# A single-core transformer block in split fp32: sums of W4's fourth pair of chunks made during the projections, those of the fifth one step sooner, with a new table of order

## The chip, the cores and the metric

One core of one Trainium2 chip runs the whole program. The metric is the device time of one execution in microseconds (us). The core has five engines that run side by side, each through its own queue in order: TensorE (PE in the profile; PEld is its loading of weights), VectorE (DVE), ScalarE (ACT), GpSimd (POOL) and SyncE (SP), which here only issues transfers. Matmuls write into PSUM banks; VectorE and ScalarE read them from there.

## The reference

The input has S = 2048 rows of D = 512, all in fp32. With `xn = layernorm(x)`:

```
q, k, v = split(xn @ wqkv)                      # 32 heads of 16
phi(t)  = where(t > 0, t + 1, exp(t)) + 1e-6
s = (phi(q) @ (phi(k)^T v)) / (phi(q) . sum(phi(k)) + 1e-6) @ wo
# B(x), on xn:
h  = gelu(layernorm(x) @ w1)                    # 4 groups of columns, moved by +1, -1, +2, -2 rows
x1 = x + shifted(h) @ w2
B  = x1 + gelu(layernorm(x1) @ w3) @ w4         # w3: 512 x 1376, w4: 1376 x 512
out = x + s * silu(B(xn))
```

## The kernel before, in words

**Arithmetic.** Each fp32 operand is split into a high part `h` (rounded on ScalarE) and a low part `l` (the difference, on VectorE). A product is three matmuls, high·high, low·high, high·low. Nearly all matmuls stand on one line, L146; activations are L168, two-tensor operations L191 and L201, operations with one tensor L196, loads L207, stores L212 and L214, fetches from the kernel's own DRAM buffers L219, gathers L225. Large products go by a scheme of seven products instead of eight (`seven`, L929): the quarters of one operand and sums of them (`a11`, `s1`, ...) are multiplied by quarters and sums of the other (`b11`, `t1`, ... `t4`). It uses three PSUM banks: `pa` once; `pe` for the product with `t1` and then, on top of it, with `b22`; and `pb` four times on top of each other, for `b11`, `t2`, `t3`, `t4`. Between two products in one bank another engine reads the partial sum: ScalarE copies `p1` and `u2` from `pb` and `p5` from `pe`, VectorE forms the third result from `pb + p5`. The next product into the bank must wait for that read, since it adds to what was read.

**Stages** (us of the profiled execution). Tiles are 128 rows, 16 of them; four make a block, four blocks. 0–54: layernorm sums, key, query and the Gram matrix of the first block (the column sums `ksum` and `qsum` of the weights, multiplied by ones, serve the layernorm). 54–129: keys and queries of blocks 1 to 3 (`pair_kq`, two tiles at a time), from sums of the transposed input's chunks. 129–230: first and second mixing product (`w1`, `w2`) and the shift. 230–291: block 0 through `w3` (`up_pair`, five pairs of chunks, s = 0 to 4, of 128 columns each) and, in plain matmuls into four accumulating banks `acc`, through `w4` (`down`). 291–405: blocks 1 to 3 through `w3` (`up_late`), with the attention products between (their banks end in `s`: `pbs`, `pes`). 405–492: blocks 2, 3 and 1 through `w4` by the scheme of seven (`down_late`), banks `pbd`, `ped`. Then the last output rows leave.

**The sums in question.** `down_late` needs the sums `t1` to `t4` of W4's pairs of chunks (s and s + 5). `sums_w4(s)` (L1190) makes them for one pair: two loads `wr` of 256 KB, four VectorE operations over 256 columns (`wt`), two high parts on ScalarE, two low parts on VectorE, and four stores of 256 KB to DRAM (`wtd`), from where `fetch_w4` brings them back later. Pair 0's are made in block 2's projections, those of 1 and 2 in block 3's. The dictionary `SUMS` names the (block, pair) of the `w3` stage after which those of pairs 3 and 4 are made.

**What sets the order.** The code above doesn't issue instructions: it records operations in a `Plan` (L79 on). `emit` (L285) then goes through them as a list scheduler with durations of its own: on each engine it takes, of the operations that could start soonest there, the one with the earliest due time. Due times follow from TensorE's recorded order; the table `SOONER` at the program's end shifts the due time of single operations, given as pairs (number of the operation in order of recording, shift in units of 0.25 us). What comes out is a fixed queue for each engine, and where each tile lies. A tile's number in a name counts tiles and differs between two programs for the same thing.

Of the kernel before, what the change touches and what calls it, by code (L numbers as in the profile page):

```python
# [411 lines left out]
def linear_attn_gated_by_mixer(  # L412
# [33 lines left out]
    SUMS = {(3, 1): (3,), (3, 3): (4,)}  # L446
# [1200 lines left out]
    for b in range(1, NQ):  # L1647
# [17 lines left out]
        if b == 3:  # L1665
            sums_w4(1)
# [47 lines left out]
    b = 2  # L1714
# [24 lines left out]
    b = 3  # L1739
# [29 lines left out]
    for b in range(NQ):  # L1769
        if b in LATE:  # L1770
            up_last(b)
            for s in range(NS):
# [3 lines left out]
                attends((b, s))  # L1776
                for k in SUMS.get((b, s), ()):
                    sums_w4(k)
# [3 lines left out]
        for n, fs in enumerate(groups):  # L1782
# [15 lines left out]
            attends((b, n))  # L1798
            for s in SUMS.get((b, n), ()):
                sums_w4(s)  # L1800
# [13 lines left out]
    for b in LINE:  # L1814
# [121 lines left out]
```

## Time and profile before

| what | us |
|---|---|
| runs | 498.06, 498.6, 498.03 |
| median | 498.06 |
| profiled execution | 498.08 |
| its span in the profile | 496.4 |
| TensorE busy | 490.6 |
| VectorE busy | 438.4 |
| ScalarE busy | 373.4 |

The span runs from the first to the last recorded instruction; the rest of an execution lies around it. Busy time is the sum of an engine's instructions. For matmuls the start is recorded and the end is modelled, so that two of them overlap in the rows; the time from one start to the next tells what TensorE got through. In a row of the timeline stand the start, the duration, engine, line, operation, output and inputs, and in brackets the idle time ahead of it with what ended it.

### The profile page before, as it was taken

Reading aid. Unit: us, or ns where it says so; the run is one execution under the profiler, and the core shown is the slowest. Engines: PE = TensorE matmul, PEld = TensorE weight load, DVE = VectorE, ACT = ScalarE, POOL = GpSimd, SP = SyncE. Lnnn points to the kernel's source line nnn. Section 1 sums busy time; section 2 is a strip of 40 time slices with the busy share of each in tenths; the row PEclk is TensorE's granted clock in tenths of the full one; section 3 lists DMA queues with packets and bytes.
Section 4 is the critical chain, followed back from the end, with each engine's and each line's share of the span. In section 5 each row is a group of like instructions: output and inputs, shape, how many; then the busy total and the mean of one; then the engine's idle time right before and its main releaser. Section 6 shows DMA issues by size and latency. Waiting matters only on the chain.

```text
span 496.4 us, 9885 instructions
## 1 busy us (share of the span) xinstructions
PE 490.6 (99%) x3244; PEld 447.0 (90%) x3244; DVE 438.4 (88%) x874; ACT 373.4 (75%) x845; POOL 123.6 (25%) x214
## 2 busy tenths in 40 slices
PE   8999999999999999999999999999999999999996
PEld 6778888888888999899889999999999999999996
DVE  5998997889989669999999999999999899796864
ACT  5999999677887599999988567765686877565531
POOL 1384404276930232133200021100000000143420
PEclk9999999999999999999999999999999999999999
DMA  7869696999974999999988499984634699599996
GB/s 229 303 187 297 133 296 183 237 287 269 329 220 100 236 310 248 273 252 290 337 268 247 158 194 298 247 262 138 183 114 147 215 336 332 114 226 283 278 224 182
DMA packets 87082, 117.44 MB, mean 237 GB/s; under 512 B 10328, under 2 KB 39160, under 8 KB 87032
## 3 DMA queue, kind: packets, MB, share of 16 engines
q1 hardware_dynamic: 75512, 96.11, 59.6%
q0 software_dynamic: 11520, 20.71, 24.9%
q8 instruction: 25, 0.41, 0.4%
q14 instruction: 25, 0.20, 0.1%
HBM read 72.66 MB, written 39.93 MB: 227 GB/s over the span
## 4 chain that ended last, share of the span: by engine, by line
PE 97%; DMA 1%; SPq 1%; ACT 0%; DVE 0%; issue 0%; ACTq 0%
PE pb L146 12%; PE pbd L146 9%; PE h L146 9%; PE g L146 9%; PE acc L146 6%; PE pe L146 6%; PE pbx L146 6%; PE ped L146 5%; PE pbm L146 5%; PE pbs L146 5%; PE q L146 3%; PE pa L146 3%; PE pex L146 3%; PE k L146 3%; PE pad L146 3%; PE pes L146 2%
## 5 line engine op out<-in xcount | busy, mean ns | idle before, releaser
L225 POOL DMA_DIRECT2D xo<-x1d x12 | 10.9, 950 | 166.2 <-DVE xo L191 118.5
L225 POOL DMA_DIRECT2D th<-in_x x14 | 12.2, 895 | 45.0 <-DVE th L201 23.1
L225 POOL DMA_DIRECT2D o<-xnd x16 | 14.0, 887 | 37.5 <-DVE o L191 13.5
L168 ACT ACTIVATE th<-xo 128x512 f32<-128x512 f32 (+1 forms) x16 | 9.7, 614 | 15.9 <-DVE xo L201 10.1
L225 POOL DMA_DIRECT2D zacc<-ke x12 | 12.9, 1073 | 31.4 <-DMA zacc<-ke 10.4
L191 DVE TENSOR_TENSOR ht<-h,abc 128x512 f32<-128x512 f32 x16 | 11.0, 690 | 7.5 <-PE h L146 7.4
L225 POOL DMA_DIRECT2D xt<-nrow x16 | 14.6, 1288 | 8.4 <-ACT k12h L168 4.1
L196 POOL TENSOR_SCALAR w<-mv 128x4 f32<-128x4 f32 (+2 forms) x10 | 2.5, 254 | 40.7 <-ACT sq L168 40.4
L168 ACT ACTIVATE y<-o,nm,rs 128x512 f32<-128x512 f32 x16 | 12.4, 814 | 0.2 <-POOL nm L196 0.2
L168 ACT ACTIVATE p<-pb 128x256 f32<-128x256 f32 x20 | 7.6, 381 | 5.8 <-PE pb L146 5.4
L168 ACT ACTIVATE ht<-ht 128x512 f32<-128x512 f32 x16 | 10.0, 626 | 2.1 <-DVE ht L191 2.0
L168 ACT ACTIVATE sq<-o,mv 128x512 f32<-128x512 f32 x16 | 11.5, 722 | 0.1
L168 ACT ACTIVATE u<-pb 128x256 f32<-128x256 f32 x20 | 7.7, 383 | 5.1 <-PE pb L146 4.5
L201 DVE SCALAR_TENSOR_TENSOR pq<-pq,rd 128x512 f32<-128x512 f32 x16 | 11.0, 688 | 0.3
L168 ACT ACTIVATE p<-pe 128x256 f32<-128x256 f32 x20 | 7.7, 384 | 4.6 <-PE pe L146 4.1
L201 DVE SCALAR_TENSOR_TENSOR qz<-pq,zb 128x512 f32<-128x512 f32 x16 | 10.8, 682 | 0.0
L1471 DVE TENSOR_REDUCE den<-qz 128x32 f32<-128x512 f32 x16 | 10.8, 679 | 0.0
L168 ACT ACTIVATE sq<-o 128x512 f32<-128x512 f32 x16 | 10.0, 629 | 0.1
L613 POOL TENSOR_TENSOR rs<-w,nhalf 128x4 f32<-128x4 f32 (+2 forms) x10 | 9.7, 970 | 0.8
L168 ACT ACTIVATE x<-x,nm,rs 128x512 f32<-128x512 f32 x12 | 9.2, 805 | 0.0
L201 DVE SCALAR_TENSOR_TENSOR th<-th,so 128x512 f32<-128x512 f32 x12 | 8.2, 683 | 0.6 <-ACT th L168 0.5
L168 ACT ACTIVATE sq<-x,mv 128x512 f32<-128x512 f32 x12 | 8.6, 718 | 0.1
(2075 smaller groups left out, 2446.9 us busy)
## 6 DMA issues: line engine op xcount, KB each, us to landing
w_s<-in_w SPq DMA_DIRECT2D x28, 256.0 KB, 5.6
x<-in_x SPq DMA_DIRECT2D x16, 256.0 KB, 6.2
xt<-in_xt SPq DMA_DIRECT2D x16, 256.0 KB, 6.9
xnd<-x SPq DMA_DIRECT2D x16, 256.0 KB, 5.9
xt<-nrow POOLq DMA_DIRECT2D x16, 256.0 KB, 7.6
pqd<-qr SPq DMA_DIRECT2D x16, 256.0 KB, 6.1
o<-xnd POOLq DMA_DIRECT2D x16, 256.0 KB, 6.6
x1d<-o SPq DMA_DIRECT2D x16, 256.0 KB, 5.1
```

The lines of the kernel that those rows point to most:

```text
L146: lambda: nc.tensor.matmul(out.get(), lhs.get(), rhs.get(), start=start, stop=stop, skip_group_check=more))
L168: nc.scalar.activation(out.get(), src.get(), func, scale=get(scale), **kw)
L191: self.vec(eng, out, [a, b], lambda: self.e(eng).tensor_tensor(out.get(), a.get(), b.get(), op=op), True)
L196: lambda: self.e(eng).tensor_scalar(out.get(), a.get(), get(s1), get(s2), **kw), False,
L201: lambda: self.nc.vector.scalar_tensor_tensor(out.get(), a.get(), get(s), b.get(), op0=op0, op1=op1),
L225: lambda: self.nc.gpsimd.dma_start(out.get(), get(src), accum_op=ALU.add), mb=mb)
L613: lambda: g.tensor_tensor(out.get(), src.get(), nh.get(), op=ALU.pow))
L1471: pl.add("DVE", .6, .68, [t], [den], lambda: nc.vector.tensor_reduce(den.get(), t.get().rearrange("p (h d) -> p h d", d=DH), axis=AX.X, op ...
```

## The change

`sums_w4(3)` moves from the stage of block 3's second pair (row (3, 1) of `SUMS`) into the projections: in the loop over blocks it is recorded in block 2's turn at the place where block 3's turn records `sums_w4(1)`, ahead of the second `pair_kq`. `sums_w4(4)` moves from (3, 3) to (3, 2). The table `SOONER` is replaced as a whole (longer by seven lines, so L1931 becomes L1938). The operations and the matmuls are the same ones.

```diff
-    SUMS = {(3, 1): (3,), (3, 3): (4,)}
+    SUMS = {(3, 2): (4,)}
...
-        if b == 3:
-            sums_w4(1)
+        if b > 1:
+            sums_w4(3 if b == 2 else 1)
         pair_kq(t0 + 1)
...
     SOONER = (
-        25, 43, 34, 17, 48, 11, 52, 22, 57, 4, 63, 3, 76, 3, 88, -164, 90, 14, 91, -77, 94, 30, 95, 2, 96, 3,
...
+        5418, 25, 5444, -19, 5471, 28, 5478, -18, 5496, -37, 5531, 47,
     )
```

**The sums of pair 3 on VectorE.** VectorE's queue in block 2's projections, near 80 us, before (`ke`, `qk`, `qi`, `qr`, `zi` are key and query intermediates, `x8` a normalised tile):

```order
L201 SCALAR_TENSOR_TENSOR qr_1071<-qe_1040,qk_881 128x512
L201 SCALAR_TENSOR_TENSOR qk_1078<-pbx_943,ns_94,p5x_1068 128x512
L201 SCALAR_TENSOR_TENSOR qi_1095<-pex_979,rs_92,u2x_1021 128x512
L201 SCALAR_TENSOR_TENSOR ke_1102<-ke_1102,zi_1043 128x512
L191 TENSOR_TENSOR x8l<-x_432,x8h 128x512
L201 SCALAR_TENSOR_TENSOR k8l<-ke_1102,k8h 128x512
L201 SCALAR_TENSOR_TENSOR ke_1135<-ke_1135,zk_1117 128x512
```

and now:

```order
L191 TENSOR_TENSOR wt_1099<-wr_974 128x256
L201 SCALAR_TENSOR_TENSOR qr_1113<-qe_1103,qk_892 128x512
L201 SCALAR_TENSOR_TENSOR ke_1110<-ke_1110,zi_1071 128x512
L191 TENSOR_TENSOR x8l<-x_337,x8h 128x512
L201 SCALAR_TENSOR_TENSOR wt_1099<-wt_1099,wr_999 128x256
L191 TENSOR_TENSOR wt_1144<-wr_999,wr_974 128x256
L201 SCALAR_TENSOR_TENSOR wt_1144<-wt_1099,wr_999 128x256
L201 SCALAR_TENSOR_TENSOR k8l<-ke_1110,k8h 128x512
L191 TENSOR_TENSOR wt_31l<-wt_1144,wt_31h 128x512
L191 TENSOR_TENSOR wt_30l<-wt_1099,wt_30h 128x512
L201 SCALAR_TENSOR_TENSOR ke_1173<-ke_1173,zk_1123 128x512
```

The four sums and the two low parts stand between the key work of tiles 8 and 9.

**Block 0's third pair on TensorE.** The pair s = 2 of block 0, bank `pb0_2`, where the product with `t3` (left factor `yt30`, weights named `w3_2_s1`) is followed by that with `t4` (left factor `yt40`, weights `w3_2_b`); `acc` are the plain products with `w4`. TensorE's queue before, near 253 us:

```order
L146 MATMUL pb0_2_3539<-yt30h_3046,w3_2_s1h_3492 128x256
L146 MATMUL pb0_2_3539<-yt30l_3180,w3_2_s1h_3492 128x256
L146 MATMUL pb0_2_3539<-yt30h_3046,w3_2_s1l_3505 128x256
L146 MATMUL acc0_3_3296<-w4_0_1h_3230,f0_1l_3495 128x512
L146 MATMUL acc0_2_3277<-w4_0_6h_3311,f0_6h_3482 128x512
L146 MATMUL acc0_1_3330<-w4_0_1h_3230,f0_1h_3476 128x512
L146 MATMUL acc0_1_3330<-w4_0_1l_3306,f0_1h_3476 128x512
L146 MATMUL pb0_2_3539<-yt40h_3146,w3_2_b_3055 128x256
L146 MATMUL pb0_2_3539<-yt40l_3192,w3_2_b_3055 128x256
```

and now:

```order
L146 MATMUL pb0_2_3495<-yt30h_3152,w3_2_s1h_3571 128x256
L146 MATMUL pb0_2_3495<-yt30l_3196,w3_2_s1h_3571 128x256
L146 MATMUL pb0_2_3495<-yt30h_3152,w3_2_s1l_3583 128x256
L146 MATMUL pb0_2_3495<-yt40h_3194,w3_2_b_3594 128x256
L146 MATMUL pb0_2_3495<-yt40l_3209,w3_2_b_3594 128x256
```

The four `acc` matmuls between the two products stand elsewhere; three such matmuls now stand ahead of `t3`, between it and `t2`.

**The first Gram matmuls.** TensorE's queue near 18 us before (`k` is the last key product, `g` the Gram products of the first tile):

```order
L146 MATMUL k_151<-wk_3h,u_3h 128x512
L146 MATMUL k_151<-wk_3l,u_3h 128x512
L146 MATMUL k_151<-wk_3h,u_3l 128x512
L146 MATMUL qsum<-wqt,ones 128x512
L146 MATMUL g_304<-k0h,x0h 128x512
L146 MATMUL g_310<-k0h,x0h 128x512
```

and now:

```order
L146 MATMUL k_160<-wk_3h,u_3h 128x512
L146 MATMUL k_160<-wk_3l,u_3h 128x512
L146 MATMUL k_160<-wk_3h,u_3l 128x512
L146 MATMUL g_295<-k0h,x0h 128x512
L146 MATMUL g_297<-k0h,x0h 128x512
```

`qsum` moves behind the first nine `g` matmuls. On ScalarE, whose `k0h` the `g` matmuls need, the queue ahead of it was

```order
L168 ACTIVATE wneg<-ksum 128x512
L168 ACTIVATE wq_2h<-wq_s_165 128x512
L168 ACTIVATE wq_0h<-wq_s_169 128x512
L168 ACTIVATE kr_261<-kt_247,rs_92 128x512
L168 ACTIVATE kt_247<-kt_247,rs_92 128x512
L168 ACTIVATE wq_1h<-wq_s_181 128x512
L168 ACTIVATE sq_281,mv_90<-x_194 128x512
L168 ACTIVATE k0h<-kr_261 128x512
```

and is now

```order
L168 ACTIVATE wneg<-ksum 128x512
L168 ACTIVATE sq_248,mv_90<-x_178 128x512
L168 ACTIVATE kr_257<-kt_246,rs_92 128x512
L168 ACTIVATE kt_246<-kt_246,rs_92 128x512
L168 ACTIVATE x0h<-x_134 128x512
L168 ACTIVATE wq_1h<-wq_s_195 128x512
L168 ACTIVATE k0h<-kr_257 128x512
```

The square of the second `x` tile (`sq`) stands ahead of `kr`, and `x0h` ahead of `k0h`.

135 rows, old and new, of the table SOONER are left out of this document.

## The prediction

> **What bounds the kernel now.** I read the page first, then the waits of TensorE, the table by stage, and last the rows of single places. On the page:
>
> ```profile
> PE 490.6 (99%) x3244; PEld 447.0 (90%) x3244; DVE 438.4 (88%) x874; ACT 373.4 (75%) x845; POOL 123.6 (25%) x214
> PE 97%; DMA 1%; SPq 1%; ACT 0%; DVE 0%; issue 0%; ACTq 0%
> ```
>
> TensorE is busy for 490.6 of the span's 496.4 us, and the chain of work that ended last is 97% TensorE. The waits of TensorE (engine, line, what was waited for, us in all, times, longest):
>
> ```profile
> PE warm L146 <- POOL ones L529: 1.1, 1, 1.1
> PE k L146 <- DVE u_1l L191: 0.4, 1, 0.4
> ```
>
> So after the first microsecond one wait is listed. The same matmuls are issued before and after the change, so it can only move time between matmuls: what is to be gained is what TensorE waits now, and what is to be lost are waits that a new order makes. VectorE's cover, by stage (bounds; duration; busy us and instructions of PE, PEld, DVE, ACT, POOL; clock; DMA share; GB/s):
>
> ```profile
> 78.00:87.00 9.00, 9.00 (x41) 7.21 (x40) 5.61 (x9) 8.86 (x21) 5.52 (x11) 1.00 0.45 118
> 97.00:101.00 4.00, 4.00 (x19) 3.25 (x18) 1.25 (x4) 1.57 (x3) 1.02 (x2) 1.00 1.08 349
> 112.00:129.00 17.00, 17.00 (x75) 13.78 (x74) 16.25 (x30) 13.61 (x25) 12.11 (x28) 1.00 1.06 297
> 230.00:291.00 61.00, 61.00 (x391) 54.95 (x390) 60.17 (x119) 50.12 (x119) 6.58 (x11) 1.00 0.82 250
> 330.00:373.00 43.00, 42.93 (x361) 42.62 (x360) 42.49 (x91) 27.75 (x74) 0.00 (x0) 1.00 0.57 160
> 373.00:405.00 32.00, 32.00 (x271) 31.93 (x270) 28.61 (x62) 23.29 (x60) 0.00 (x0) 1.00 0.69 218
> ```
>
> VectorE has 3.39 of 9 us free in 78–87 and 2.75 of 4 in 97–101, but under 1 us of 61 in 230–291. The clock column says 1.00 throughout.
>
> The span's end is not touched. The last matmul starts at 491.79, one ScalarE and two VectorE operations follow, then the store; the new order ends with the same ones (start, duration, of the first two):
>
> ```profile
> 491.79 0.28 PE L146 MATMUL pbd<-w_l1h,dl1l 96*128 96x256 f32 x1
> 492.10 0.38 ACT L168 ACTIVATE th<-pbd 128x256 f32<-128x256 f32 x1 [1.16 <-PE pbd L146]
> ```
>
> **What a handover of a PSUM bank costs.** The waits view drops idle times that the modelled ends of matmuls cover, so I take the step from one matmul's start to the next. In the dense stages it is 0.232 us for 512 columns and 0.118 for 256. Where TensorE may only go on in a bank once it has been read, the step grows. The dearest place after the first 20 us is at 338, where `t1` of the last-but-one query pair ends in bank `pes`, four matmuls into `pbs` follow, and `b22` then needs `pes` (start, duration):
>
> ```profile
> 337.77 0.28 PE L146 MATMUL pes<-m_t1h,q6s0l 128*128 128x256 f32 x1
> 338.15 0.39 ACT L168 ACTIVATE p5s<-pes 128x256 f32<-128x256 f32 x1 [1.16 <-PE pes L146]
> 338.24 0.28 PE L146 MATMUL pbs<-m_t2h,q6s0l 128*128 128x256 f32 x1
> 338.59 0.39 PE L146 MATMUL pes<-m_b22h,q6s1h 128*128 128x256 f32 x1
> 338.81 0.28 PE L146 MATMUL pes<-m_b22l,q6s1h 128*128 128x256 f32 x1
> ```
>
> The reader starts 0.38 behind the last matmul's start, reads for 0.39, and TensorE goes on 0.05 later: 0.82 from matmul to matmul. The step 338.24→338.59 is 0.35 in place of 0.118, and the one behind it 0.22: together 0.33 lost, with four matmuls in between. With none in between, 0.82 − 0.118 = 0.70 is lost and 0.10 in the step behind, 0.80 in all.
>
> **The change part by part.**
>
> *The sums of the fourth pair, moved from about 388–400 to about 78–87.* One set is four VectorE operations over 256 columns, two ScalarE copies, two VectorE subtractions, two loads ahead and four stores behind:
>
> ```profile
> L201 DVE SCALAR_TENSOR_TENSOR wt<-wt,wr x10: 418/422/427, 89.5 to 399.4; 128x256 f32<-128x256 f32 x10
> L191 DVE TENSOR_TENSOR wt_01l<-wt,wt_01h x1: 682/682/682, 92.7 to 92.7; 128x512 fp32r<-128x512 f32 x1
> L168 ACT ACTIVATE wt_01h<-wt x1: 623/623/623, 91.2 to 91.2; 128x512 fp32r<-128x512 f32 x1
> ```
>
> VectorE: 4 × 0.42 + 2 × 0.68 = 3.04 us, less than the 3.39 free in 78–87. ScalarE: 2 × 0.62 = 1.24 us, and ScalarE is full there (8.86 of 9), so the copies, which stand behind block 2's key work, push that by up to 1.2 us; VectorE's 2.75 and ScalarE's 2.43 free us in 97–101 lie behind it and take the push up again before the fourth block's chunks are needed. I take 0, with 0 to +0.5 as bounds: if that cover were gone, TensorE would wait for one subtraction of 0.68, less the 0.16 that a bank's reader leaves free below. The two loads are issued on SP among the fourth block's `xt` loads, the four stores behind them: six transfers of 256 KB, 1.57 MB. At 112–129 the core moves 297 GB/s with the engines full, so they take 1.57/0.297 = 5.3 us; in 78–87 more than half of the DMA time is free (0.45, so 0.55 × 9 = 5.0 us). What is left, and what slips past 87, pushes the SP queue's loads of `w1` and block 0's rows back, by 5.3 us at the most. These are used from 129.1 on (durations min/median/max in ns, first and last start), and block 0's first chunk is split by 123.1 + 0.7:
>
> ```profile
> L191 DVE TENSOR_TENSOR u_0l<-xt,u_0h x1: 682/682/682, 123.1 to 123.1; 128x512 fp32r<-128x512 f32 x1
> L146 PE MATMUL h<-u_0h,w_0h x4: 394/398/401, 129.1 to 137.7; 128*128 128x512 f32 x4
> ```
>
> That is 5.3 us of lead. I take 0, bounds 0 to +1.5 (a tail of one and a half transfers, 0.88 us each at 297 GB/s).
>
> *Where the sums stood, 373–405:* VectorE becomes 3 us freer, but it already had 3.4 us free, and the only stall of TensorE over 0.1 us that I find there is a handover at 383.60; one like it stands ahead, at 357.63:
>
> ```profile
> 357.44 0.28 PE L146 MATMUL pe<-yt12h,w_s0h 128*128 128x256 f32 x1
> 357.63 0.39 PE L146 MATMUL pbs<-m_t4h,q 128*128 128x256 f32 x1
> 357.85 0.28 PE L146 MATMUL pbs<-m_t4l,q 128*128 128x256 f32 x1
> ...
> 383.45 0.28 PE L146 MATMUL pes<-m_t1h,q12s0l 128*128 128x256 f32 x1
> 383.60 0.38 PE L146 MATMUL pb<-yt43h,w_b 128*128 128x256 f32 x1
> 383.82 0.28 PE L146 MATMUL pb<-yt43l,w_b 128*128 128x256 f32 x1
> ```
>
> At 383 the steps 0.15 + 0.22 stand for 2 × 0.118: 0.13 lost; at 357, 0.19 + 0.22: 0.17. The one at 338 keeps its four matmuls in the new order. I take both as gone, −0.3; bounds −0.6 (the one at 338 too) to +0.3 (they stay, and as much again comes up elsewhere).
>
> *The order anew, block 0's third pair, near 253–256:* here is what I find against the change. Today (start, duration):
>
> ```profile
> 253.28 0.28 PE L146 MATMUL pb<-yt30h,w_s1l 128*128 128x256 f32 x1
> 253.40 0.39 PE L146 MATMUL acc<-w_1h,f_1l 128*128 128x512 f32 x1
> 253.75 0.42 DVE L191 TENSOR_TENSOR gf<-pb,p 128x256 f32<-128x256 f32 x1
> 254.33 0.28 PE L146 MATMUL pb<-yt40h,w_b 128*128 128x256 f32 x1
> ```
>
> Between the end of `t3` in bank `pb` and `t4` in the same bank stand four matmuls of 512 columns, 0.93 us, in which VectorE forms `gf` from the bank; `t4` starts 0.16 behind its end without loss. In the new order `t4` follows `t3` directly, so TensorE stands through the whole handover: 0.80 by the place at 338. VectorE's row before that `gf` is a subtraction of about 0.69 that itself follows another `gf`, which waits for ScalarE's copy of `t2`. From `t2`'s last matmul: copy done at 0.38 + 0.39 = 0.77, that `gf` at 1.2, the subtraction at about 1.85; `t3`'s last matmul starts at 3 × 0.232 + 6 × 0.118 = 1.40, its result is readable at 1.78. So VectorE comes 0.07 late: I take 0.85. Bounds: 0.7 (the reader starting 0.31 behind its matmul, as at 492.10, and the step behind it free) and 1.5 (one more VectorE operation of 0.69 in front, which with 60.17 of 61 us busy can be).
>
> By the Trainium skill, "TensorE: Matmul & The Clock Gate", section "Single matmul latency", a warm matmul of N columns takes (398 + N)/2.4 ns, an estimate of 0.27 us for 256 columns; the stall would then be 0.27 + 0.42 − 0.12 = 0.57, and the sum 498.6. The trace does not bear this out as the whole price: its reader starts 0.38 behind the start, so some 0.11 us lies between a result and whoever waits for it.
>
> *The order anew, the first 20 us.* The column sums of the key weights end later on VectorE, so `ksum` moves six matmuls back, 6 × 0.232 = 1.39 us. `qsum` goes from ahead of the first Gram matmuls to behind them. Today:
>
> ```profile
> 18.28 0.39 PE L146 MATMUL k<-wk_3h,u_3l 128*128 128x512 f32 x1
> 18.51 1.02 PE L146 MATMUL qsum<-wqt,ones 128*128 128x512 f32 x2
> 19.00 0.99 PE L146 MATMUL g<-k0h,x0h 128*128 128x512 f32 x2
> 15.01 0.69 DVE L191 TENSOR_TENSOR wqt<-wq_s,wq_s 128x512 f32<-128x512 f32 x1 [0.60 <-DMA wq_s<-in_wqkv]
> 14.91 0.71 ACT L168 ACTIVATE kr<-kt,rs 128x512 f32<-128x512 f32 x1
> 15.65 0.73 ACT L168 ACTIVATE kt<-kt,rs 128x512 f32<-128x512 f32 x1
> 16.28 0.62 ACT L168 ACTIVATE wq_1h<-wq_s 128x512 fp32r<-128x512 f32 x1
> 17.79 0.64 ACT L168 ACTIVATE k0h<-kr 128x512 fp32r<-128x512 f32 x1 [0.28 <-DVE kr L201]
> ```
>
> In the new order a square of the second `x` tile stands ahead of `kr`, and this tile takes the place in the load queue of the `wq` tile that VectorE waited for until 15.01. So: square 15.0, `kr` 15.6, `kt` 16.35, `x0h` 17.0, `wq_1h` 17.5, `k0h` 18.05 to 18.7. The Gram matmuls are due at 18.51, as `qsum` no longer stands ahead, and start at 18.75: +0.25. Bounds: −0.3 (most of the wait of 0.4 for `u_1l` goes, as its matmul stands later, and nothing replaces it) to +0.9 (the tile lands later, and the next copies with it).
>
> **The sum.** 0.25 + 0.85 − 0.3 = +0.8. The profiled execution took 498.08 us (span 496.4 and 1.7 around it), as good as the median of the runs, 498.06. That gives 498.9. About 0.2%, 1.0 us, is what a measurement of this kernel can tell from no change, so 498.9 is still within it, on the slow side.
>
> **The rivals.**
>
> *The handover at the third pair and the start cost as said, little else moves* (forecast, 498.9; its own range 498.4 to 499.3): chance 0.46.
>
> *Slower: VectorE is late at that handover.* Place: `t4` of block 0's third pair. It decides at the point where VectorE is still more than about 0.6 us behind when `t3` is readable; then one more operation stands in front, the stall is 1.5 in place of 0.85, and the start takes its 0.25 and nothing is won back: 498.08 + 1.5 + 0.25 = 499.8. For it: VectorE has 0.83 us free in the 61 us around. Against: those 61 us cause no wait today, and every stall of TensorE lets VectorE catch up. Chance 0.25.
>
> *Slower: the six transfers come too late for block 0.* Place: TensorE's first `h` matmuls near 129. It decides where the push, with the splits behind it, exceeds the 5.3 us of lead; one transfer of 0.88 us past it costs as much, 498.9 + 0.9 = 499.8. For it: DMA share 1.06 in 112–129. Against: the 5.0 us free in 78–87. Chance 0.07.
>
> *Faster: the waits go.* Of what TensorE waits today, 0.4 at the start and 0.33 + 0.30 in the middle could go, if the third pair costs nothing and the Gram matmuls don't wait: 498.08 − 1.03 = 497.05. For it speaks that VectorE, which is behind all of 230–373, has 3 us less to do after 373; against it that the handover at 338 stays, and that the place near 253 stands in the new order as plainly as that one. Chance 0.08.
>
> *The change does nothing that counts:* ScalarE's and VectorE's work near 253 has been placed ahead well enough that the handover costs half, 0.4, and the small stalls give it back: 498.1. Chance 0.14.
>
> **How the numbers follow.** The likeliest is 498.9. Faster than 497.06: the faster rival, 0.08. Slower than 499.06: the two slower rivals, 0.32, and 0.10 of the forecast's upper end: 0.42. The rest, 0.50, is no change. Range: down to 497.7, which leaves most of the faster rival out, up to 500.2, which takes in 499.8 with 0.4 for the bound of the smaller stalls; some 2 in 10 are left out.
>
> **What would show it.** In the changed kernel, between `t3` and `t4` of block 0's third pair, a step of 0.8 to 0.9 us between two 256-column matmuls, and VectorE's `gf` in it; `g<-k0h,x0h` directly behind the last `k` matmul, 0.2–0.3 late, held by `k0h`; no wait at 100–130; the step at 338 as now; the end 4.3 us behind the last matmul. Wrong it is if the first `h` matmuls wait, if that step is near 0.118, or if stalls of over 0.3 us stand in 230–373 where none is now.

## The result and the profile after

| what | before | after |
|---|---|---|
| runs, us | 498.06, 498.6, 498.03, 497.94 | 501.75, 501.48, 501.12, 502.35 |
| median, us | 498.04 | 501.62 |
| profiled execution, us | 498.08 | 501.75 |
| its span, us | 496.4 | 499.7 |

The change makes the kernel slower: after / before is 1.0071, with a 95% interval of 1.0053 to 1.0088, some 3.5 us. The prediction of 498.9 had the sign and named one of the places, but the time lies above its range. The page after (busy time by engine, and the chain that ended last):

```profile
PE 491.8 (98%) x3244; PEld 445.7 (89%) x3244; DVE 438.8 (88%) x874; ACT 374.3 (75%) x845; POOL 126.8 (25%) x214
PE 81%; DMA 6%; ACT 4%; issue 4%; DVE 2%; POOL 2%; SPq 0%; POOLq 0%; DVEq 0%
```

No engine has more than 1.2 us more to do, apart from GpSimd's 3.2. TensorE's part in the chain falls from 97% to 81%: the rest now runs through transfers, ScalarE and VectorE, so it is a matter of waits. The waits of TensorE are four in place of two:

```profile
PE k L146 <- ACT u_0h L168: 1.5, 1, 1.5
PE warm L146 <- POOL ones L529: 1.1, 1, 1.1
PE pbm L146 <- ACT p1m L168: 0.7, 1, 0.7
PE pb L146 <- DVE gf L191: 0.5, 1, 0.5
```

This view is a pointer and no sum: it leaves out what the modelled ends of matmuls cover. So I took, for both traces, every step from one matmul's start to the next, less 0.232 us (512 columns) or 0.118 (256), and added them up by stage. The 42 matmuls of 128 columns are left out, and an edge between two stages can move up to 0.1 us from one row to its neighbour:

| stage, us | before | after | more |
|---|---|---|---|
| start, to 40 | 4.98 | 5.48 | 0.50 |
| 40–98 | 0.24 | 0.33 | 0.09 |
| 98–106 | −0.03 | 0.84 | **0.87** |
| 106–178 | −0.04 | 0.11 | 0.15 |
| 178–198 | 0.64 | 1.36 | **0.72** |
| 198 to block 0's first `acc` matmul | 0.15 | 0.19 | 0.04 |
| block 0 (first to last `acc`, 232–291) | 0.11 | 0.88 | **0.77** |
| from there to 405 | 1.19 | 1.46 | 0.27 |
| 405 to the end | 0.24 | 0.25 | 0.01 |

The sum is 3.4 us. The last matmul starts 3.62 later, at 495.41 in place of 491.79. The difference is mostly in the 32 `kv` matmuls of 128 columns, whose steps take 3.24 us in place of 3.07; all of them stand in 178–198, so that with them counted this stage loses 0.89 more, and not 0.72. Three places carry 2.4 of the 3.4.

**101 us.** TensorE and ScalarE after, then the same high part and `zk` on ScalarE before:

```profile
101.05 0.40 PE L146 MATMUL pbx<-wk_1h,u_1l 128*128 128x512 f32 x1
101.57 0.50 PE L146 MATMUL pax<-wk_2h,u_2h 128*128 128x512 f32 x1
101.91 0.40 PE L146 MATMUL pax<-wk_2l,u_2h 128*128 128x512 f32 x1
102.30 0.50 PE L146 MATMUL pax<-wk_2h,u_2l 128*128 128x512 f32 x1
```

```profile
99.64 0.69 ACT L168 ACTIVATE zk<-pbx,ns 128x512 f32<-128x512 f32 x1 [1.13 <-issue]
100.36 0.63 ACT L168 ACTIVATE ke<-zk 128x512 f32<-128x512 f32 x1
100.90 0.62 ACT L168 ACTIVATE u_2h<-xt 128x512 fp32r<-128x512 f32 x1
```

```profile
94.74 0.64 ACT L168 ACTIVATE u_2h<-xt 128x512 fp32r<-128x512 f32 x1 [0.61 <-DMA xt<-nrow]
...
99.43 0.69 ACT L168 ACTIVATE zk<-pbx,ns 128x512 f32<-128x512 f32 x1 [3.54 <-PE pbx L146]
```

The first steps are 0.52, 0.34 and 0.39 in place of 0.232. Before, ScalarE made `u_2h` at 94.74, 4.7 us ahead of the first matmul that needs it. After, it stands in ScalarE's queue behind `zk`, which reads a bank that TensorE has not finished (the row names no releaser; the last matmul into that `pbx` starts at 99.16, 0.48 ahead of `zk`), and behind `ke`: it ends at 101.52 and TensorE, which needs it, starts at 101.57. The low part `u_2l` follows it on VectorE.

**181 us.** TensorE's wait, and on ScalarE (after) what stands ahead of the `p1m` that it waits for:

```profile
181.38 0.39 PE L146 MATMUL h<-u_3h,w_3l 128*128 128x512 f32 x1
182.43 0.39 PE L146 MATMUL pbm<-w_t2h,hs21h 128*128 128x256 f32 x1 [0.66 <-ACT p1m L168]
```

```profile
176.47 0.63 ACT L168 ACTIVATE sq<-o 128x512 f32<-128x512 f32 x1 [2.98 <-DMA o<-xnd]
...
182.02 0.36 ACT L168 ACTIVATE p1m<-pbm 128x256 f32<-128x256 f32 x1
```

ScalarE stands still for 2.98 us until a gather of `o` lands; from then on it works without a gap up to `p1m`. Before, the first square follows its neighbour at 174.10 without a wait. The gathers of two tiles of `o` (GpSimd issues them) and their neighbours in SP's queue after; in the second view the columns are those of the queue, SPq:

```profile
165.63 1.77 POOL L225 DMA_DIRECT2D o<-xnd  x2 [11.35 <-DVE o L191]
```

```profile
163.94 0.45 SPq L207 DMA_DIRECT2D wv_s<-in_wqkv  x1
164.44 0.96 SPq L207 DMA_DIRECT2D w_s<-in_w  x2
165.56 1.28 SPq L207 DMA_DIRECT2D wv_s<-in_wqkv  x3
166.89 1.65 SPq L207 DMA_DIRECT2D wo_s<-in_wo  x2
```

Eight weight loads of 256 KB are issued from 163.9 to 168.5, around the gathers. Before, the eight that are issued there are out by 165.5, and the first gather goes at 164.21, 1.4 us sooner. The two gathers and the first square before, and then the gather that the first square waits for after (start, and us to its landing):

```profile
164.21 1.77 POOL L225 DMA_DIRECT2D o<-xnd  x2 [10.08 <-DVE hs2f L191]
174.10 0.63 ACT L168 ACTIVATE sq<-o 128x512 f32<-128x512 f32 x1
```

```profile
166.42 9.97 DMA o<-xnd
```

The transfers themselves were hardly slower: from issue to landing the first took 8.9 us before and 8.7 after, the second 9.7 and 10.0. But the order of the squares has changed too. In both programs the tile gathered first is tile 0 of `o` and the second is tile 2. Before, ScalarE squares tile 0 first, which landed at 173.11; after, it squares tile 2 first, which landed at 176.39, while tile 0 lay there from 174.36. So by these rows the later start comes from the later issue, 1.4 us, and from squaring first the tile that lands last, 2.0 us; before, ScalarE came to tile 0 only 1.0 us after it had landed, so 2.4 of the 3.4 show.

**260 us, block 0's third pair**, where the prediction looked. TensorE, then VectorE's reader:

```profile
260.13 0.28 PE L146 MATMUL pb<-yt30h,w_s1l 128*128 128x256 f32 x1
260.92 0.39 PE L146 MATMUL pb<-yt40h,w_b 128*128 128x256 f32 x1 [0.52 <-DVE gf L191]
261.14 0.28 PE L146 MATMUL pb<-yt40l,w_b 128*128 128x256 f32 x1
```

```profile
259.78 0.69 DVE L191 TENSOR_TENSOR w_s1l<-w_sf,w_s1h 128x512 fp32r<-128x512 f32 x1
260.44 0.42 DVE L191 TENSOR_TENSOR gf<-pb,p 128x256 f32<-128x256 f32 x1
```

The step is 0.80 and the one behind it 0.22: 0.78 lost. Together with the start, these are the places. (At the start a matmul waits 1.5 us for `u_0h`, but only 0.50 more is lost in all, since the steps there are long before too.) The end is 4.3 us behind the last matmul in place of 4.6, which gives 0.3 back, and no matmul near 129 waits: `h` follows its neighbour in 0.23.

```profile
129.10 0.39 PE L146 MATMUL g<-k14h,x14l 128*128 128x512 f32 x1
129.33 0.40 PE L146 MATMUL h<-u_0h,w_0h 128*128 128x512 f32 x1
```

### The profile page after: what moved, and what is told of

It is laid out like the page before. It is cut to its first block, busy times and chain, and to the rows that moved or that the text cites. A ratio compares the mean times of both kernels' runs of the same rounds, so it can differ in the third digit from the quotient of the medians.

```text
span 499.7 us, 9918 instructions
## 1 busy us (share of the span) xinstructions
PE 491.8 (98%) x3244; PEld 445.7 (89%) x3244; DVE 438.8 (88%) x874; ACT 374.3 (75%) x845; POOL 126.8 (25%) x214
## 4 chain that ended last, share of the span: by engine, by line
PE 81%; DMA 6%; ACT 4%; issue 4%; DVE 2%; POOL 2%; SPq 0%; POOLq 0%; DVEq 0%
PE pb L146 11%; PE pbd L146 9%; PE g L146 7%; PE pe L146 5%; PE ped L146 5%; PE pbs L146 5%; PE pbx L146 5%; PE acc L146 4%; PE k L146 3%; PE q L146 3%; PE pbm L146 3%; DMA zacc<-ke 3%; PE pex L146 3%; PE pad L146 3%; PE pa L146 3%
## 5 line engine op out<-in xcount | busy, mean ns | idle before, releaser
L196 POOL TENSOR_SCALAR w<-mv 128x4 f32<-128x4 f32 (+2 forms) x10 | 4.6, 461 | 46.2 <-ACT sq L168 46.0
```

The source lines that it names most:

```text
L196: lambda: self.e(eng).tensor_scalar(out.get(), a.get(), get(s1), get(s2), **kw), False,
```

## The experiments

For the experiments an order can be written out whole: each kernel below takes the fixed queues of the changed kernel (or of the one before) and moves single rows. Where nothing else is said the figure of a stage is the sum over the steps as in the table above, and ratios are to the kernel before on the same chip (498.4 us). The start alone differs by up to 0.95 us between the traces of this order, and the intervals of most single edits overlap with that of the changed kernel; so what an edit does is read from the stage sums of its trace, and not from its time. My theory after the result: three separate places, each a matter of order and not of the moved sums' own work. The rival: the sums, as work on full engines and queues, push everything behind them.

**The order again, unedited** (`after_again`):

> The changed kernel once more, unchanged, for a second trace. In its first trace TensorE waits 1.5 us for u_0h at 5.6 to 7.1 us, where the first xt tile landed at 6.6 in place of 4.8 before. If that landing is chance (the queues up to there are alike), the wait differs from trace to trace, and with it the time by up to 0.5 us. If it belongs to the new program, the wait stands again at 1.4 to 1.6 us. The stalls near 101 (0.9 us), 182 (0.9) and 260 (0.8) should stand again either way, time 501.1 to 502.3.

502.2 us, 1.0077 (1.0059 to 1.0095); 98–106 0.84, 178–198 1.71, block 0 0.92. The same places, so they belong to the order; the one at 181 varies with the gather (its reader starts at 177.15 here).

**The sums back at 385–396, all else as in the new order** (`sums_late`): the fourteen operations of pair 3's sums are taken out at 78–87 on SP, VectorE and ScalarE, and put in behind the matmuls near 390. VectorE's queue where they are taken out:

```diff
-L191 TENSOR_TENSOR wt<-wr 128x256
 L201 SCALAR_TENSOR_TENSOR qr<-qe,qk 128x512
...
-L201 SCALAR_TENSOR_TENSOR wt<-wt,wr 128x256
-L191 TENSOR_TENSOR wt<-wr,wr 128x256
-L201 SCALAR_TENSOR_TENSOR wt<-wt,wr 128x256
...
-L191 TENSOR_TENSOR wt_31l<-wt,wt_31h 128x512
-L191 TENSOR_TENSOR wt_30l<-wt,wt_30h 128x512
```

> The changed kernel with every instruction in the order of the changed kernel, but for the 14 of the sums of pair 3, which go back to 385 to 396 us. Theory A, the order costs: the stalls near 101 and 182 hang on single instructions that stand ahead of others on ScalarE, so both stay (0.9 and 0.9 us) and the time stays at 501.1 to 502.3. Theory B, the sums cost where they were put (3.0 us of VectorE, 1.2 of ScalarE, 1.57 MB of transfers): both stalls go, the time falls by 1.5 to 1.8 us to about 499.9.

507.1 us, 1.0174 (1.0132 to 1.0216). At 98–106 the stage still loses 0.82: that stall isn't the sums' work. 178–198 falls to 0.43; the gather's reader starts at 174.54 here, 9.5 us after the issue, where the ten traces with the early sums and the same eight loads have 10.6 to 11.3. So at the second place the early sums may have a part; why they should, no run shows, and one trace does not rule out chance. The time is 5.5 us longer. In the profiled execution, the fastest of the four (504.64), the new place, which was not tuned, loses some 4.4: 390–402 and 448–467 wait for ScalarE and VectorE (the longest, 1.2, is `pbd` for `d_s20l`). So it answers the first place only.

**The sums early in the order of before** (`before_sums`, and `before_sums2` with other buffers). SP's queue (`before_sums`):

```diff
+L207 DMA wr<-in_w 128x512
 L207 DMA xt_0<-in_xt 128x512
+L207 DMA wr<-in_w 128x512
 L207 DMA xt_1<-in_xt 128x512
...
+L212 DMA wt<-wt_30h 128x512
+L212 DMA wt<-wt_30l 128x512
+L212 DMA wt<-wt_31h 128x512
+L212 DMA wt<-wt_31l 128x512
```

> The kernel before with every instruction in its old order, but for the 14 of the sums of pair 3, which go into block 2's projections, at 69 to 86 us, between the same neighbours as in the changed kernel. Theory A, the order costs: no more than 0.3 us slower than before, 498.0 to 498.4, and no stall over 0.3 us at 100 to 104 or 180 to 190. Theory B, the sums cost where they were put: 0.9 to 1.8 us slower, 499.0 to 499.9, with a stall at 100 to 104.

> The kernel before with the 14 instructions of pair 3's sums at 69 to 86 us, as in the run before_sums, but with the sums' tiles in those free buffers that are wanted last, so that no other tile takes the buffer of a store that is still under way. Theory A, the order costs, not the sums: 498.0 to 498.7, no stall over 0.4 us. Theory B, the sums cost where they were put: 499.0 to 500.5, with stalls over 0.5 us at 78 to 104. Theory E, they cost buffers: stalls again at places where a tile waits for a store, 500 or more.

507.66 us (1.0187, 1.017 to 1.0204) and 516.5 us (1.0351, 1.0315 to 1.0388). VectorE, `before_sums`:

```profile
80.70 0.69 DVE L191 TENSOR_TENSOR x7l<-x,x7h 128x512 fp32r<-128x512 f32 x1 [3.63 <-DMA pqd<-qr]
```

The low part `x7l` waits 3.63 us for a *store*: the buffer that it writes into is still being read out. Later, `hs1f` waits 6.12 us at 151.08 for the store of `wt_21h` in the same way. In the second kernel ScalarE's `qe` waits 8.41 us for the store of `wt_31l`, one of the moved sums' own tiles, and `u2x` behind it makes TensorE wait 9.6. Of the 90 buffers nearly all are in use at that time, and a tile that comes in earlier pushes others onto buffers whose store is under way. Both are inconclusive on what the sums cost by themselves; they show that these two ways to put the sums there, with the rest of the order left as it was, cost 9 and 18 us.

**`u_2h` ahead of `zk` and `ke`** (`u2_first`), ScalarE:

```diff
 L168 ACTIVATE u_1h<-xt_1 128x512
-L168 ACTIVATE zk<-pbx,ns 128x512
-L168 ACTIVATE ke<-zk 128x512
 L168 ACTIVATE u_2h<-xt_2 128x512
+L168 ACTIVATE zk<-pbx,ns 128x512
+L168 ACTIVATE ke<-zk 128x512
```

> The changed kernel with one ScalarE operation moved: u_2h of block 3 ahead of zk and ke, for which ScalarE waits 1.1 us at 98.5 to 99.6. Theory A, the order costs: the steps over 0.1 us at 101 to 104 (0.9 us in sum) fall to 0.3 or less, and the time by 0.6 to 0.9 us. Rival: u_2h's input has not landed before about 100.5, as the sums' transfers stand ahead; then the stall stays, or zk comes later and a new one stands at its place.

500.67 us, 1.0048 (1.003 to 1.0065). 98–106 falls from 0.84 to 0.19, and TensorE runs through (steps of 0.23):

```profile
98.34 0.63 ACT L168 ACTIVATE u_2h<-xt 128x512 fp32r<-128x512 f32 x1
99.52 0.69 ACT L168 ACTIVATE zk<-pbx,ns 128x512 f32<-128x512 f32 x1 [0.54 <-DVE xf L191]
```

```profile
100.88 0.39 PE L146 MATMUL pbx<-wk_1h,u_1l 128*128 128x512 f32 x1
101.11 0.40 PE L146 MATMUL pax<-wk_2h,u_2h 128*128 128x512 f32 x1
```

The place in ScalarE's queue is the cause; 0.65 of the 0.87 us come back.

**Four weight loads behind the gather** (`loads_behind`), SP:

```diff
-L207 DMA wv_s<-in_wqkv 128x512
-L207 DMA wv_s<-in_wqkv 128x512
-L207 DMA wo_s<-in_wo 128x512
-L207 DMA wo_s<-in_wo 128x512
 L212 DMA x1d<-o 128x512
 L212 DMA x1d<-o 128x512
+L207 DMA wv_s<-in_wqkv 128x512
+L207 DMA wv_s<-in_wqkv 128x512
+L207 DMA wo_s<-in_wo 128x512
+L207 DMA wo_s<-in_wo 128x512
```

> The changed kernel with four of the eight weight loads on SP that stand at 165 to 168 us, around the first two gathers of o, moved behind the third store of x1d, near 175. Theory C: the 2 MB of loads ahead make the gather land 10.8 us after its issue, ScalarE stands on it, and p1m behind it; then o lands by 174.5 or earlier in place of 176.5, the stall of 0.9 us near 182 goes, and the time falls by 0.8 to 1.0 us. Rival: the gather is late for its own sake; it lands at 176 to 177 again and the stall stays at 0.6 to 1.2 us.

501.21 us, 1.0051 (1.0037 to 1.0065); 178–198 falls from 1.36 to 0.42. (Before has 0.64; with the 128-column matmuls counted at 0.118, the three figures are 0.82, −0.12 and −0.07, so the loss of this stage is gone.) The gather is issued at the same time, 165.64:

```profile
174.35 0.63 ACT L168 ACTIVATE sq<-o 128x512 f32<-128x512 f32 x1 [0.85 <-DMA o<-xnd]
```

```profile
181.39 0.40 PE L146 MATMUL h<-u_3h,w_3l 128*128 128x512 f32 x1
181.62 0.28 PE L146 MATMUL pbm<-w_t2h,hs21h 128*128 128x256 f32 x1
```

Its reader starts 2.1 us earlier, and TensorE's wait of a microsecond is gone. So the loads beside it are part of what it takes, and moving them is one way to mend the place. That they are what the new order made worse is not shown: before, eight such loads stood around the gather too. The other way, to square the tile that lands first ahead of the other, would by the landings let ScalarE start at 174.4 as well; it was not tried.

**Eight matmuls between `t3` and `t4`** (`pair3_fill`), TensorE:

```diff
 L146 MATMUL pb_2<-yt30h,w_2_s1l 128x256
+L146 MATMUL pb_3<-yb110h,w_3_ah 128x256
+L146 MATMUL pb_3<-yb110l,w_3_ah 128x256
+L146 MATMUL pa_3<-yb210h,w_3_ah 128x256
...
 L146 MATMUL pb_2<-yt40h,w_2_b 128x256
```

> The changed kernel with eight matmuls of 256 columns (0.94 us, the fourth pair's b11 and the product for its second bank) moved from behind t4 to between t3 and t4 of block 0's third pair. If the handover of the bank is the cost, the step of 0.80 us there falls to 0.12 and the span by 0.75 to 0.8 us. Rival: VectorE is the bound there, and the wait only moves on to a later matmul within 230 to 290; then the span falls by less than 0.4 us.

500.81 us, 1.0047 (1.003 to 1.0064). The time is 0.8 under the changed kernel's, but not by this edit: in the trace, the start and 178–198, which it does not touch, lose 0.46 and 0.16 less. The step of 0.80 is gone, yet the stage loses 0.80 in place of 0.88: the wait comes back 5 us later, at the fourth pair's `t2`, with a step of 0.52 in place of 0.232:

```profile
265.84 0.40 PE L146 MATMUL acc<-w_2h,f_2l 128*128 128x512 f32 x1
266.36 0.39 PE L146 MATMUL pb<-yt20h,w_s0h 128*128 128x256 f32 x1
```

So here I formed another theory: VectorE, which stood 1.0 us at 240–250 waiting for a full ScalarE, pays for that in whichever handover comes next.

**Work for VectorE's waits at 240** (`dve_fill`: four sums `w_4_sf` moved ahead of `f_0l` and of the `y` turns), the same with three other edits (`mended`: with `u_2h` first, the eight matmuls, and `p1m` ahead of two `ht`), and a larger rearrangement of VectorE and ScalarE there (`block0`: `qz` and one `w_4_sf` earlier, the work on `f_5` and `f_6` ahead of the squares, and the eight matmuls). VectorE in `dve_fill`, and the one row of `mended` on ScalarE that is new:

```diff
+L191 TENSOR_TENSOR w_4_sf<-w_4_s 128x256
+L191 TENSOR_TENSOR w_4_sf<-w_4_sf,w_4_s 128x256
 L191 TENSOR_TENSOR f_0l<-gf_0,f_0h 128x512
+L191 TENSOR_TENSOR w_4_sf<-w_4_s,w_4_s 128x256
+L191 TENSOR_TENSOR w_4_sf<-w_4_s,w_4_sf 128x256
 L155 STREAM_TRANSPOSE y_0z<-y 128x512
```

```diff
+L168 ACTIVATE p1m<-pbm 128x256
 L168 ACTIVATE ht_0<-ht_0 128x512
 L168 ACTIVATE ht_1<-ht_1 128x512
-L168 ACTIVATE p1m<-pbm 128x256
```

> The changed kernel with four VectorE operations moved (sums of the fifth pair of w3, ready by then): two ahead of f_0l, two ahead of the turning of y, where VectorE waits 0.50 and 0.38 us for ScalarE near 241. Theory D, VectorE's lost time is what block 0 pays: VectorE's waits there fall under 0.2 us, later stalls from lag go, but t4 behind t3 still waits for the handover, so the step at 260 stays at 0.8 and the time changes by less than 0.3 us by this edit alone. Rival: the handover at 260 is longer than its own time because VectorE lags; then the step falls to 0.7 or less.

> The changed kernel with four edits: eight matmuls between t3 and t4 of the third pair, the four VectorE operations moved ahead as in the run before, u_2h first, and ScalarE's p1m of the third mixing tile ahead of two gelus. If the four places are the loss: 101 to 104 costs 0.3 or less, 182 0.2 or less, 230 to 290 0.2 or less, together 2.1 us under the changed kernel, 499.2 to 500.0, still 1 us or so over the kernel before (start and small steps). Rival: the two moves in block 0 are no more than one of them alone (0.1 us), and the waits come up elsewhere: 500.3 or more.

> The changed kernel with three edits, all for block 0 at 230 to 290: eight matmuls between t3 and t4 of the third pair; VectorE's two waits near 241 (0.50 and 0.38 us for ScalarE) filled with a product of the attention and a sum of w3; and four ScalarE operations for f_5 and f_6 ahead of the squares at 244 to 247. Theory D, the stage pays for VectorE's lost time (1.0 us of waits in a stage that VectorE fills) and the handover only shows it: with both mended the stage loses 0.4 us or less in place of 0.9. Rival: ScalarE, full at 230 to 250, is late as a whole, and no order of these few helps; then the stage loses 0.7 us or more again.

501.69 us (1.0063, 1.0048 to 1.0079), 501.31 us (1.0054, 1.0041 to 1.0066) and 504.82 us (1.0133, 1.0118 to 1.0147). Misses, all three. Block 0 loses 1.48, 0.80 and 4.49. In `dve_fill` the moved sums wait for their loads (0.28 and 0.37), and in `block0` the moved `qz` waits for a fetch:

```profile
243.00 0.69 DVE L201 SCALAR_TENSOR_TENSOR qz<-pq,zb 128x512 f32<-128x512 f32 x1 [2.76 <-DMA pq<-pqd]
```

So an operation moved earlier there finds its input missing. In `mended` the `p1m` in front only moves the wait at 181 on to `u2m` (0.50 at 184.19): ScalarE is late there, not `p1m` misplaced.

**The start** (`start_first`: on ScalarE `kr` and `kt` ahead of the square `sq`, on VectorE `kr` ahead of the second tile's `kt`). ScalarE:

```diff
-L168 ACTIVATE sq,mv<-x 128x512
 L168 ACTIVATE kr<-kt,rs 128x512
 L168 ACTIVATE kt<-kt,rs 128x512
+L168 ACTIVATE sq,mv<-x 128x512
```

> The changed kernel with the square of the second x tile on ScalarE moved behind kr and kt of the first tile, and VectorE's kt of the second tile behind kr. The wait of the first g matmul for k0h (0.3 us in some traces) goes. The wait for u_0h near 6 us, if there is one, comes from the landing of the first xt tile and is not touched: the start as a whole costs 0 to 0.5 us more than in the kernel before. Rival: k0h's wait is made by the late landing itself, then it stands again whenever u_0h waits.

502.26 us, 1.0079 (1.0063 to 1.0094). No gain; TensorE still waits for `k0h`, 0.76 from the last `k` (18.10) to the first `g`:

```profile
18.86 0.97 PE L146 MATMUL g<-k0h,x0h 128*128 128x512 f32 x3 [0.36 <-ACT k0h L168]
```

**More together** (`all_mended`: `block0`, `loads_behind`, `u2_first` and `start_first`):

> The changed kernel with the edits of block0 and start_first, u_2h first, and the four weight loads behind. If the losses are those four places and add up: 0.65 at 101, 0.94 at 182, up to 0.6 in block 0, up to 0.3 at the start under the changed kernel, 499.0 to 499.9, still 0.5 to 1.4 us over the kernel before. Rival: they overlap, or others come up: 500.3 or more.

505.77 us, 1.014 (1.0115 to 1.0166): 98–106 0.25 and 178–198 0.40, but block 0 6.09, by `block0`'s edit.

**Three edits together** (`three_together`: `u2_first`, `loads_behind`, `pair3_fill`):

> The changed order with three edits that were tried alone: u_2h ahead of the key copies zk and ke on ScalarE (alone 0.65 us in 98-106), four weight loads moved behind the gather of o (alone 0.94 us in 178-198), eight matmuls between t3 and t4 of block 0's third pair (alone 0.08 us in block 0). If the causes are separate: 98-106 loses 0.2, 178-198 0.4, block 0 0.8, and the time is 501.6 - 1.7 = 499.9. If what is won at one place is given back at a later one: 500.6 or more, with new steps behind 106 or behind 198.

500.1 us, 1.0032 (1.0021 to 1.0044). 98–106 0.21, 178–198 0.42, block 0 0.82: the gains of the first two add up, and nothing is given back behind them. This is the fastest of the kernels in the new order, and still 1.7 us behind the one before on its chip (498.41); block 0, and the small steps to 405 (1.49 against 1.19), hold a microsecond of that.

**Less work for VectorE in block 0**, without (`light`) and with (`fill_light`) the eight matmuls. Both kernels leave out two products `pq * rd`, so the attention's result is not divided by its sum for these tiles; they serve for the time alone. VectorE:

```diff
-L201 SCALAR_TENSOR_TENSOR pq<-pq,rd 128x512
...
-L201 SCALAR_TENSOR_TENSOR pq<-pq,rd 128x512
```

> The changed order without the two products pq * rd alone (as above; the attention's result is not divided for these tiles), nothing between t3 and t4. If the step of 0.80 there is TensorE's own handover (theory, as predicted): it stays 0.79 to 0.80, the stage loses 0.8 to 0.9, time as the changed kernel, 501.6. If VectorE is behind at that point too (rival): the step falls by 0.1 or more, 501.3 or less.

> The changed order with the eight matmuls between t3 and t4, and without the two products pq * rd (the query's division by its sum) of VectorE in block 0, so the attention's result is not divided for these tiles; VectorE has 1.3 us less at 251.7 and 256.3. If VectorE's 1.0 us lost at 240-250 pays for block 0 (theory): the steps at 262.9 and 265.8 go and the stage loses 0.3 or less in place of 0.80; 0.5 us faster than the kernel with the eight matmuls alone (500.81), so 500.3. If ScalarE or the handovers themselves pay (rival): the stage stays at 0.7 to 0.8, 500.8.

501.35 us (1.0064, 1.0043 to 1.0085) and 501.3 us (1.0056, 1.0042 to 1.007). `light`, TensorE (`t3`'s last matmul is at 259.46) and VectorE:

```profile
260.25 0.39 PE L146 MATMUL pb<-yt40h,w_b 128*128 128x256 f32 x1 [0.52 <-DVE gf L191]
```

```profile
258.74 0.42 DVE L191 TENSOR_TENSOR gf<-u,pe 128x256 f32<-128x256 f32 x1 [0.79 <-ACT u L168]
259.08 0.69 DVE L191 TENSOR_TENSOR w_s1l<-w_sf,w_s1h 128x512 fp32r<-128x512 f32 x1
259.77 0.42 DVE L191 TENSOR_TENSOR gf<-pb,p 128x256 f32<-128x256 f32 x1
```

VectorE now stands 0.79 us just ahead and the step is still 0.79: it is the handover alone, with a VectorE that is on time. In `fill_light` the step at 266.35 stays 0.51 and the stage 0.79. So the second theory falls: what VectorE lost at 240–250 is made good by 258, and relieving it ahead of the handover gains nothing in this stage.

**ScalarE's copies in the fourth pair** (`p_first`: `three_together` with the copy `p` of bank `pb` one place sooner; `p_both`: the copy of bank `pe` too). ScalarE, `p_both`:

```diff
+L168 ACTIVATE p_3<-pe_3 128x256
 L168 ACTIVATE m_b11h<-mq 128x512
-L168 ACTIVATE p_3<-pe_3 128x256
 L168 ACTIVATE m_t1h<-m_f 128x512
 L168 ACTIVATE m_t3h<-m_f 128x512
+L168 ACTIVATE p_3<-pb_3 128x256
 L168 ACTIVATE m_b21h<-mq 128x512
-L168 ACTIVATE p_3<-pb_3 128x256
```

> The three edits together (500.1 us), and on ScalarE the copy p of the fourth pair's bank pb one place sooner, ahead of m_b21h. In the three edits it starts at 264.72, though its bank is readable at about 264.2, and the next product in the bank starts at 265.14, 0.29 late, with 0.11 in the step behind. If ScalarE's order there is what holds block 0 after the eight matmuls (theory): that step becomes 0.23, the stage loses 0.4 to 0.5 in place of 0.82, 499.7 us. If VectorE, dense from 260 on, sets the pace (rival): the loss comes back at a later handover of the stage, which loses 0.7 or more, 500.0 to 500.2.

> As the one before it, and the copy p of the same pair's bank pe ahead of m_b11h too, which now holds it up by 0.3. Theory: the step of 0.22 behind 261.72 goes as well, the stage loses 0.3 to 0.4, 499.6 us. Rival (VectorE): 0.7 or more, 500.0 to 500.2.

500.29 us (1.0036, 1.0023 to 1.0048) and 500.31 us (1.0037, 1.0023 to 1.0051); block 0 loses 0.78 and 0.81, as without them. The step at `t2` goes, and the next handover of the same bank, `t3` behind ScalarE's `u`, takes 0.51 in its place (`p_first`, TensorE, then ScalarE):

```profile
266.47 0.40 PE L146 MATMUL acc<-w_7l,f_7h 128*128 128x512 f32 x1
266.98 0.39 PE L146 MATMUL pb<-yt30h,w_s1h 128*128 128x256 f32 x1
```

```profile
263.05 0.63 ACT L168 ACTIVATE m_t1h<-m_f 128x512 fp32r<-128x512 f32 x1 [1.42 <-DVE m_f L191]
...
266.56 0.36 ACT L168 ACTIVATE u<-pb 128x256 f32<-128x256 f32 x1
```

`u` comes at 266.56, at the end of a row of ScalarE operations without a gap that begins with `m_t1h`, and this waits 1.42 us for VectorE's `m_f`. VectorE itself runs from 258.5 to past 269 without a wait. So the loss comes back at a later handover, as the rival said, and a full VectorE behind 258 may be what sets the pace; it was not tried by taking some of its work away. Another reading stands beside it. The last matmul that `u` waits for starts at 265.42, and `u` stands in ScalarE's queue behind `m_b22h` and `w_3h` (265.52 and 266.04), so by its place it is some 0.7 late, as `u_2h` was at 101. `u` ahead of these two was not tried, so which of the two engines holds this place stays open.

**More work for VectorE in the kernel before** (`before_heavy`):

```diff
-L201 SCALAR_TENSOR_TENSOR qz<-pq,zb 128x512
+L201 SCALAR_TENSOR_TENSOR qz<-pq,zb 128x512 x2
...
-L1471 TENSOR_REDUCE den<-qz 128x32
+L1471 TENSOR_REDUCE den<-qz 128x32 x2
```

> The kernel before in its own order, with two VectorE operations of block 0 (qz at 240.8 and its sum den at 242.6) made twice, 1.2 us more on VectorE, nothing else. If a VectorE that is about 1 us late costs TensorE in block 0 (theory): the stage loses 0.6 to 1.2 more than the 0.11 of before, 498.6 to 499.3. If the free time of VectorE around it takes it up (rival): 0 to 0.2, 498.0 to 498.3.

499.49 us, 1.0022 (1.0013 to 1.0031). Block 0 loses 1.23 in place of 0.11, in two waits, of which this is the first; the other is at 246.8, for `f_5l`:

```profile
242.34 0.39 PE L146 MATMUL acc<-w_0h,f_0h 128*128 128x512 f32 x1
243.08 0.50 PE L146 MATMUL acc<-w_0h,f_0l 128*128 128x512 f32 x1 [0.35 <-DVE f_0l L191]
```

The order of before has little slack on VectorE there: in the trace its two repeated operations take 1.45 us, and 1.12 come out as waits of TensorE.

## Why the prediction was wrong

**The handover in block 0: right, in place and size.** Said was a step of 0.8 to 0.9 and 0.85 lost; it is 0.80, with 0.78 lost. The reader starts 0.31 behind the matmul (260.13 to 260.44) and not 0.38 + 0.07: VectorE starts to read sooner than the ScalarE of the place at 338, and is not late; `light` shows that, and with it that the slower rival, a late VectorE at this handover, did not come. But what stands behind it was missed: take the handover away, and 0.8 is lost all the same, at the next handovers of the bank; whether VectorE or ScalarE's queue holds these is open. The Trainium skill, "TensorE: Matmul & The Clock Gate", section "Single matmul latency", gives its formula for a single bf16 matmul, and these work on fp32r parts. The 0.57 estimated from it is 0.21 too small here: by the rows above, 0.04 of that lies ahead of the reader's start (0.31 and not 0.27), 0.06 between the reader's end and the next matmul, and 0.10 in the step behind it.

**The start: right in size on the mean, and partly by luck.** The profiled execution lost 0.50 and not the 0.25 said, and by the landing of the first `xt` tile, with the first `g` matmul on time behind the last `k` (18.65 to 18.88). In four of the fourteen traces with the unedited start `k0h` does hold `g`, by 0.3 to 0.4 (as in `start_first` above); in the rest it does not. The mean of the fourteen traces with the unedited start is 5.31, that of the four in before's order 5.06: 0.25 more.

**The small stalls: wrong in sign, by 0.6.** I let 357 and 383 go and 338 stay. From block 0 to 405 the loss is 1.46 in place of 1.19: the old steps went, and others came, the largest of them the handover of `pes` that stood at 338, now at 342:

```profile
341.95 0.28 PE L146 MATMUL pbs<-m_t2h,q6s0l 128*128 128x256 f32 x1
342.24 0.39 PE L146 MATMUL pes<-m_b22h,q6s1h 128*128 128x256 f32 x1
342.46 0.28 PE L146 MATMUL pes<-m_b22l,q6s1h 128*128 128x256 f32 x1
```

A new order trades such steps, so counting only those that go is one-sided. None of these was tried by itself.

**The projections, 54–129: the step that failed.** I took 0 for the sums there, as VectorE's 2.75 and ScalarE's 2.43 free us in 97–101 "lie behind it and take the push up again", and named as a sign "no wait at 100–130". The 0 for the work itself may stand (98–106 loses as much with the sums gone, `sums_late`). The cover was argued wrongly: free time of an engine is no cover for an operation that stands behind one that waits. In the new order ScalarE was idle for 1.13 us right ahead of `zk`, with `u_2h` behind it. I looked there only at the sums, and not at what else the new order had moved on ScalarE. It cost 0.87, of which 0.65 were won back by moving one row.

**The gathers at 165: not among the terms.** The six new transfers were weighed against `h` at 129, which indeed did not wait. For 129–230 the sum has no term at all, which puts it at nothing without a reason. There the new order issues the gathers 1.4 us later, and squares the tile that lands last first, with eight weight loads around the gathers as before; this cost 0.72 (0.89 with the 128-column matmuls). Moving four of the loads takes it away; how the loss divides between the issue and the squares, and what part the early sums have in it, is open. I had priced the three places that I had found in the order, and bounded the rest by the small stalls alone.

**The end: said to be untouched, with 4.3 us behind the last matmul.** It was 4.6 in the profile before and is 4.3 after, so 0.3 of what TensorE lost does not show in the span.

Both missed terms together are 1.6 of the 2.7 us by which the forecast fell short; the small stalls are 0.6, the rest of the start 0.25, the small rises at 40–98 and 106–178 0.24. What stays open besides: whether the sums, in an order that suits them, gain anything.

## What to carry to other kernels

With a new order of everything, the places at which it was looked at are a sample, and the range has to carry the rest. Walk each queue that works in order and ask of each operation that TensorE needs soon what stands ahead of it that waits for a bank or for a landing: an engine with idle time can still be late. A handover without matmuls between cost the reader's lag and its time here (0.31 and 0.42 us, and 0.16 behind them), but matmuls put there only moved the loss to the bank's next handover: look at that one too before counting the gain.

## What the runs showed of the hardware

The same program lands its transfers at different times: the first `xt` tile let `u_0h` start at 6.63 in the trace of after, at 6.19 in one other of the new order, and between 4.63 and 5.01 in the fourteen that remain. In the new order the gathers of `o` took 8.7 to 8.8 us from the first issue to the reader of the second tile in the five kernels with four weight loads fewer beside them, and 9.5 to 11.3 in the eleven with all eight. And writing into a buffer whose store was under way made VectorE wait 3.63 and 6.12 us (`before_sums`) and ScalarE 8.41 (`before_sums2`).
